# Attention, max-of-three layer and gated layer on one core: two weight pairs put together in PSUM banks of the row products, half products in other banks, every second output copy on ScalarE

## The chip, the cores and the metric

One core of a Trainium2 chip runs the whole program once. The metric is device time in microseconds (us), the median of several runs. The engines of the core are named as the profile names them: PE (TensorE, the matrix unit; PEld is its weight load), DVE (VectorE), ACT (ScalarE), POOL (GpSimd) and SP (SyncE, which here only issues DMAs). Matrix products land in PSUM, of which there are eight banks of 128 x 512 fp32; everything else lies in SBUF.

## The reference, cut to what matters

Attention over 2 batches, 8 heads, 768 positions and head width 64, in which a query sees the 8 global positions and the 96 positions behind it; then a layer with the largest of three products; then a normalised, gated layer.

```python
scores = np.matmul(q, k.transpose(0, 1, 3, 2)) / np.sqrt(64)
# keep = (pos < n_global) | ((0 <= rel) & (rel < n_local)); a bias falls linearly with distance
a = softmax(where(keep, scores + bias, -1e9))
x = np.matmul(a, v)                                   # as 1536 tokens x 512

h = np.maximum(np.maximum(x @ w1, x @ w2), x @ w3)    # 512 -> 768
x = h @ w_out                                         # 768 -> 512

xn = x / sqrt(mean(x * x) + 1e-6) * rms_g
g, val = xn @ w_gate, xn @ w_val                      # 512 -> 1536
out = (g / (1 + exp(-g)) * val) @ w_out2              # 1536 -> 512
```

## The kernel before

**Numbers.** Every fp32 operand of a large product is held as two parts, a rounded one and the rest (`op[:, 0]`, `op[:, 1]`), and a product is three matrix products of such parts. The weights come as 64-bit numbers and are put together on the chip: `scaled` (L131) lets ACT scale the high words into a buffer `x`, and `bits` (L148) has three DVE steps, L152 (shift), L154 (or with the low words, `raw`) and L160 (sign). The buffer of the first two steps is a PSUM bank where `self.psx` is set (its tile is then called `xs`) and SBUF otherwise.

**Stages.** (1) Attention, 24 units `d` (a pair of heads, 256 queries) in rounds, with the first products of the second layer (`mm`, L473) put in between. Per round DVE does the normaliser `rs` (L1095, L1096), a copy `xf` of an older unit's output out of PSUM (L1153), four score rows with their maximum (L1083), a copy `at` (L1120) and one or two weight steps; ACT does four exponentials (L1087), the copies `xt` (L1148) and `at` (L1118) and weight steps; POOL scales the probabilities (L1101), takes `xt`'s rest (L1155) and splits weights (L174). (2) The remaining products of the max-of-three layer, by a scheme with seven products in place of eight (`chained`, L689), 49 of them. (3) `behind` (L893): twelve row products `mo` of 18 matmuls (L558), each 128 tokens wide. Before one runs, its hidden rows are split by `row_part` (L538): ACT casts (L542), then DVE (part 0, and part 1 of the first row) or POOL (part 1 of the others) takes the rest `rst` (L544). After one has run, ACT squares it (L571), DVE averages (`ms`, L576), POOL takes the root (`ri`, L578), DVE scales (`x`, L582), PE transposes (`tr`, L592), and DVE, ACT and POOL make seven sums of it (`xb`, L596 to L613). (4) `gated`: 14 half products `q` for the first hidden block (`second`, L619), then 77 products `c` (L703), then the output products `acc` (L820) and stores.

**Order.** In the stages 1, 2 and 4 the order on each engine is the program's. In stage 3 only PE keeps it; the other engines are placed by a planner, from the same dependences. Between the stages 2 and 3 DVE also holds `sums1` (L711), which closes the last maximum `h_1` (L733 to L755) that row 0 needs.

**What the change touches.** `pace` (L119) takes one more step of weight work, `operand` (L302) splits one of the seven combinations of a weight pair (ACT L314, POOL L315), and `mixed` (L271) first forms four of these by sums (L282; on POOL for the max-of-three weights, on DVE for gated ones, numbered `f` >= 0). In stage 3 the banks come from `single` (L442), six of them in three pools of two; `bank` (L438) gives one of two other banks, used there for the transposes.

## Time and profile before

| | us |
|---|---|
| median of 3 runs (566.63 to 568.32) | 566.73 |
| the profiled execution's own time | 566.71 |
| its span, first to last instruction | 564.8 |
| PE busy | 546.7 (97%) |
| DVE busy | 381.4 (68%) |
| ACT busy | 292.0 (52%) |
| POOL busy | 314.7 (56%) |

The granted TensorE clock was 0.998 of full speed over the span. The page's slices show where PE is not full: PE stands at 9 tenths in nearly all of 40 slices and at 6 in the one slice from 226 to 240 us, where stage 2 ends and stage 3 starts; DVE stands at 9 there and in the slices from 14 to 56 us. A row of a timeline gives the start, the busy time, the engine, the line and the tile written and read; what stands in brackets is how long the engine sat idle before it and what ended that.

### The profile page before, as it was taken

The page shows a single profiled execution, that of the slowest core. Times are in us where ns is not written, and L with a number is a line of the kernel's source. Part 1 is how long each engine was busy: PE and PEld are TensorE (multiplying, and loading weights), DVE is VectorE, ACT ScalarE, POOL GpSimd, SP SyncE. Part 2 cuts the span into 40 slices and gives each one's busy share as a digit, 9 for nine tenths or more (in the row PEclk, how much of TensorE's full clock was granted, in tenths as well). Part 3 has the DMA queues.
Part 4 walks back from the last instruction along what each step waited for, and adds up shares of the span by engine and source line. Part 5 has one row for each costly group of instructions (what it writes and reads, how often), then busy time and mean ns, then how long its engine had stood idle before and what let it go on. Part 6 is the DMA issues. An engine that isn't in the chain of part 4 may idle for free.

```text
span 564.8 us, 9257 instructions
## 1 busy us (share of the span) xinstructions
PE 546.7 (97%) x3240; PEld 495.2 (88%) x3240; DVE 381.4 (68%) x788; ACT 292.0 (52%) x684; POOL 314.7 (56%) x397
## 2 busy tenths in 40 slices
PE   8988999999999999699999999999999999999995
PEld 4667887899999999588899999999999998888884
DVE  5999899578767768977687555555556359662220
ACT  4887768445644552566565555554444455442210
POOL 4679688666755771676746666666666527320000
PEclk9999999999999999999999999999999999999999
DMA  8666551102422432220001122222222205203101
GB/s 295 209 227 196 165 202 39 38 1 75 149 76 75 126 99 75 75 75 1 0 1 29 54 72 72 76 75 74 76 75 74 75 5 180 77 1 131 38 20 43
DMA packets 15896, 48.74 MB, mean 86 GB/s; under 512 B 2016, under 2 KB 2016, under 8 KB 15840
## 3 DMA queue, kind: packets, MB, share of 16 engines
q1 hardware_dynamic: 15840, 48.05, 26.5%
q8 instruction: 28, 0.46, 0.3%
q14 instruction: 28, 0.23, 0.1%
HBM read 44.90 MB, written 3.15 MB: 85 GB/s over the span
## 4 chain that ended last, share of the span: by engine, by line
PE 81%; DVE 14%; ACT 2%; issue 1%; POOL 1%; DVEq 0%; ACTq 0%; POOLq 0%
PE c L703 28%; PE acc L820 17%; PE mo L558 7%; PE mm L473 4%; DVE s L1083 3%; PE sc L1070 2%; PE av L1134 2%; PE tr L1111 2%; PE c_-2_0_2680 L703 1%; PE c_-3_0_2529 L703 1%; PE c_-4_0_2384 L703 1%; PE c_-5_0_2229 L703 1%; PE c_-6_0_2078 L703 1%; PE c_-7_0_1966 L703 1%; DVE x L160 1%
## 5 line engine op out<-in xcount | busy, mean ns | idle before, releaser
L703 PE MATMUL c<-xb,op 128*128 128x384 f32 x924 | 160.4, 334 | 0.2 <-DVE g L645 0.2
L703 PEld LDWEIGHTS c<-xb,op 128*128 128x128 f32 x924 | 160.1, 188 | 0.5 <-POOL op L315 0.5
L315 POOL TENSOR_TENSOR op<-s,op 128x256 fp32r<-128x256 f32 x48 | 39.3, 821 | 32.6 <-ACT op L314 31.5
L558 PE MATMUL mo<-w,rst 128*128 128x512 f32 x216 | 52.7, 396 | 2.9 <-DVE rst L544 2.9
L1101 POOL TENSOR_SCALAR s<-s,rs 128x232 f32<-128x232 f32 (+1 forms) x96 | 41.8, 454 | 20.3 <-DVE rs L1096 11.1
L1087 ACT ACTIVATE s<-s,nmx 128x232 f32<-128x232 f32 (+1 forms) x96 | 44.5, 466 | 14.4 <-DVE nmx L1083 14.2
L558 PEld LDWEIGHTS mo<-w,rst 128*128 128x128 f32 x216 | 39.6, 188 | 11.7 <-issue 2.1
L820 PE MATMUL acc<-w,gst 128*128 128x512 f32 x216 | 49.2, 389 | 0.0
L820 PE MATMUL acc<-w,st 128*128 128x512 f32 x216 | 49.1, 389 | 0.0
L820 PEld LDWEIGHTS acc<-w,st 128*128 128x128 f32 x216 | 40.5, 188 | 8.4
L820 PEld LDWEIGHTS acc<-w,gst 128*128 128x128 f32 x216 | 40.5, 188 | 8.4
L174 POOL TENSOR_TENSOR w<-x,w 128x512 fp32r<-128x512 f32 x22 | 32.3, 1466 | 26.7 <-ACT w L171 26.7
L315 POOL TENSOR_TENSOR op<-x,op 128x256 fp32r<-128x256 f32 x36 | 28.9, 806 | 28.9 <-ACT op L314 27.6
L769 POOL TENSOR_TENSOR h<-h,g 128x768 f32<-128x768 f32 x20 | 36.9, 1847 | 12.3 <-ACT g L787 10.0
L152 DVE TENSOR_SCALAR xs<-xs 128x512 int32<-128x512 int32 x48 | 33.2, 691 | 8.7 <-ACT xs L140 8.5
L790 DVE TENSOR_TENSOR h<-c,h 128x768 f32<-128x768 f32 x11 | 10.5, 957 | 41.8 <-PE c L703 41.8
L473 PE MATMUL mm<-xt,w 128*128 128x384 f32 x192 | 37.7, 343 | 0.6 <-ACT h L488 0.6
L160 DVE SCALAR_TENSOR_TENSOR x<-raw,xs 128x512 int32<-128x512 int32 x48 | 32.8, 684 | 2.9
L1070 PE MATMUL sc<-qk 64*128 64x232 f32 (+1 forms) x192 | 28.8, 377 | 5.7 <-DVE nmx L1083 5.4
L473 PEld LDWEIGHTS mm<-xt,w 128*128 128x128 f32 x192 | 32.6, 188 | 1.3 <-ACT h L488 1.0
L154 DVE SCALAR_TENSOR_TENSOR xs<-raw,xs 128x512 int32<-128x512 int32 x48 | 33.1, 690 | 0.9
L1083 DVE CUSTOM_DVE_ANT_0 s<-sc,bias 128x232 f32<-128x232 f32 (+1 forms) x96 | 31.5, 375 | 0.6 <-PE sc L1070 0.2
(453 smaller groups left out, 1108.4 us busy)
## 6 DMA issues: line engine op xcount, KB each, us to landing
raw<-wgv SPq DMA_DIRECT2D x24, 512.0 KB, 3.6
raw<-w SPq DMA_DIRECT2D x18, 512.0 KB, 3.9
raw<-wo SPq DMA_DIRECT2D x18, 512.0 KB, 3.6
qk<-qk SPq DMA_DIRECT2D x24, 312.0 KB, 4.0
v<-vwin SPq DMA_DIRECT2D x10, 512.0 KB, 4.7
out<-o SPq DMA_DIRECT2D x12, 256.0 KB, 2.1
v<-vwin SPq DMA_DIRECT2D x2, 256.0 KB, 3.9
gcol<-gcol SPq DMA_DIRECT2D x1, 2.0 KB, 1.6
```

The lines of the kernel that those rows point to most:

```text
L152: nc.vector.tensor_scalar(x, x, 3, 0x7FFFFFFF, op0=ALU.logical_shift_left, op1=ALU.bitwise_and)
L160: nc.vector.scalar_tensor_tensor(out=self.x[i].bitcast(I32), in0=raw[:, :, 1], scalar=-(1 << 31), in1=x, op0=ALU.bitwise_and, op1=ALU.bitw ...
L315: nc.gpsimd.tensor_tensor(out=t[:, 1, :], in0=s, in1=t[:, 0, :], op=ALU.subtract)
L473: self.nc.tensor.matmul(ps, w[:, wi, k * P:(k + 1) * P], x[b][:, k, xi, c0:c0 + C2], start=(i == 0), stop=(i == 3 * KT - 1),)
L558: self.nc.tensor.matmul(ps, h[:, k % 3, hi, :], w[:, wi, :], start=(k + x == 0), stop=(k == NF1 - 1 and x == 2),)
L703: nc.tensor.matmul(two[:, b, :C2], a[:, wi, k * P:(k + 1) * P], x, start=(i == 0 and j in (0, 1, 5)), stop=(i == 5), skip_group_check=True,)
L769: nc.gpsimd.tensor_tensor(out=o, in0=o, in1=y, op=ALU.mult)
L820: self.nc.tensor.matmul(ps, of(si), w[:, wi, :], start=(f == LAST[0] and si == 1), stop=(f == LAST[-1] and si == 0 and wi == 0),)
L1070: nc.tensor.matmul(sc[j][:, i, :n], qk[r, i * P:(i + 1) * P], qk[r, k0:k0 + n], start=True, stop=True)
L1083: nc.vector.tensor_tensor_reduce(out=s[:, j, :n], in0=self.sc[d][j][:, i, :n], in1=self.bias(n, 2 * pr + j), scale=-QK, scalar=3.0e38, op0 ...
L1087: nc.scalar.activation(s[:, j, :n], s[:, j, :n], AF.Exp, bias=nmx[:, j:j + 1], scale=-1.0, accum_out=sm[:, i, j:j + 1])
L1101: nc.gpsimd.tensor_scalar(s[:, j, :n], s[:, j, :n], rs[:, i, j:j + 1], 1.0, op0=ALU.mult, op1=ALU.mult)
```

## The change

There are five edits. The attention's `xf` copies of odd units go from DVE to ACT. The weight buffers `x` come from one pool of four instead of two pools of two. In `behind`, weight pairs 1 and 2 (gate and value) are put together in a PSUM bank of the first of the three row-product pools (`psx` with tag `m1`), pair 1 from the third row on and pair 2 from the sixth, instead of in SBUF from the first row on; pair 0's seven operands are appended to `order` and issued there too. The sums of pair 0 go from DVE to POOL (`f <= 0`). And in `second` the last two products of the second half (`j > 4`) take their banks from `bank`, with the rotation of the two-bank pools started one further (`n_bank = 1`).

```diff
@@ -101,11 +101,11 @@
         e = ctx.enter_context
         self.rawp = e(tc.tile_pool(name="rawp", bufs=NRAW))
         self.sp = e(tc.tile_pool(name="sump", bufs=3))
-        self.xp = [e(tc.tile_pool(name="xp0", bufs=2)), None]
+        self.xp = e(tc.tile_pool(name="xp", bufs=4))
         self.ops = self.psx = self.xone = None
         self.w, self.places, self.x, self.raws = {}, {}, {}, {}
         self.done, self.held, self.in_psum = set(), set(), set()
-        self.blocked, self.mix = False, {}
+        self.blocked, self.mix, self.psx_tag = False, {}, "mm"
         self.run = self.everything()
 
     def __getitem__(self, key):
@@ -132,7 +132,7 @@
 
 
         if self.psx is not None:
-            x = self.psx.tile([P, 512], F32, tag="mm", name=f"xs_{i}")
+            x = self.psx.tile([P, 512], F32, tag=self.psx_tag, name=f"xs_{i}")
             self.in_psum.add(i)
         else:
             x = self.xof(i).tile([P, 512], F32, tag="x", name=f"x_{i}")
@@ -140,10 +140,7 @@
         self.nc.scalar.activation(x, self.raws[i][:, :, 1].bitcast(F32), AF.Copy, scale=2.0 ** -112)
 
     def xof(self, i):
-        key, _, place = self.units[i]
-        if place == "wo1":
-            return self.xone
-        return self.xp[(key[1] if place == "op" else i) % 2]
+        return self.xone if self.units[i][2] == "wo1" else self.xp
 
     def bits(self, i, part):
         nc = self.nc
@@ -278,7 +275,7 @@
 
         def of(x, y, op):
             s = self.sp.tile([P, h], F32, tag="s", name=f"s_{f}_{j}")
-            eng = self.nc.gpsimd if -NA < f < 0 else self.nc.vector
+            eng = self.nc.gpsimd if -NA < f <= 0 else self.nc.vector
             eng.tensor_tensor(out=s, in0=x, in1=y, op=op)
             return s
 
@@ -343,7 +340,6 @@
             {q: xtp.tile([P, 2, C2], F32, tag=f"xf{b}{q[0]}{q[1]}", name=f"xf_{b}{q[0]}{q[1]}") for q in QUARTERS}
             for b in range(B)
         ]
-        self.weights.xp[1] = e(tc.tile_pool(name="xp1", bufs=2))
         self.ring_only = ExitStack()
         ring = self.ring_only.enter_context(tc.tile_pool(name="ring", bufs=RING))
         self.weights.places["ring"] = (ring, "w")
@@ -400,7 +396,6 @@
         self.thi_one.close()
         self.two_only.close()
         self.weights.psx = None
-        self.weights.xp[1] = self.ctx.enter_context(self.tc.tile_pool(name="xp2", bufs=2))
         e, tc = self.rows_only.enter_context, self.tc
         self.singles = [e(tc.tile_pool(name=f"m1{n}", bufs=2, space=PSUM, side="right")) for n in range(3)]
         self.rowp = e(tc.tile_pool(name="rowp", bufs=4, side="right"))
@@ -418,7 +413,7 @@
         self.rows_only.close()
         self.open_twos()
         e, tc = self.ctx.enter_context, self.tc
-        self.weights.psx = self.mm0
+        self.weights.psx, self.weights.psx_tag = self.mm0, "mm"
         h2b = e(tc.tile_pool(name="h2b", bufs=1, side="right"))
         self.h2.append(h2b.tile([P, NF1, NT], F32, tag="h", name="h2_2"))
         self.weights.places["wo2a"] = (e(tc.tile_pool(name="wo2a", bufs=1, side="right")), "wo2")
@@ -624,7 +619,7 @@
         a = self.weights["op", f, j]
         for b in range(b0, b1):
             later.step()
-            ps = self.single("q_" + nm, C2)
+            ps = (self.bank if b and j > 4 else self.single)("q_" + nm, C2)
             i = 0
             for k in range(2):
                 for wi, xi in ((1, 0), (0, 1), (0, 0)):
@@ -841,7 +836,8 @@
     def next_op(self):
         if self.n_op < len(self.order):
             self.n_op += 1
-            self.weights.operand(*self.order[self.n_op - 1], (self.order + [None])[self.n_op])
+            then = None if self.n_op in (self.n_first, len(self.order)) else self.order[self.n_op]
+            self.weights.operand(*self.order[self.n_op - 1], then)
 
     def begin(self):
 
@@ -851,6 +847,8 @@
         for o in range(1 - NA, z):
             self.order += [(o, 0), (o - 1, 4), (o - 1, 6), (o, 1), (o, 2), (o, 5), (o, 3)]
         self.order += [(z, 0), (z - 1, 4), (z, 2), (z - 1, 6), (z, 3), (z, 5), (z, 1), (z, 6), (z, 4)]
+        self.n_first = len(self.order)
+        self.order += [(0, j) for j in range(7)]
 
     def strassen(self):
 
@@ -873,10 +871,10 @@
         later.flush()
         self.open_strassen()
         self.rst, done = {}, 0
-        for n, (o, j) in enumerate(self.order):
+        for n, (o, j) in enumerate(self.order[:self.n_first]):
             later.step()
             for b, _ in enumerate(self.chained(o, j)):
-                if b == 0:
+                if b == 0 and self.n_op < self.n_first:
                     self.next_op()
                 h = 2 * (n % 7) + b + 1
                 paces = min(-(-PACES[n // 7] * max(h - 2 * (n < 7), 0) // (8 if n < 7 else 10 if PACES[n // 7] == 6 else 14)), PACES[n // 7])
@@ -895,22 +893,21 @@
 
         w = self.weights
         self.open_second()
-        n_op = 0
         for t in range(NT // P):
+            w.psx, w.psx_tag = self.singles[0], "m1"
             for n, _ in enumerate(self.rows(t)):
-                if ("x", 1) in w.done and n_op < 7:
-                    w.operand(0, n_op)
-                    n_op += 1
-                elif ("x", 2) not in w.done:
+                if t > (1 if ("x", 1) not in w.done else 4) and ("x", 2) not in w.done:
                     w.pace()
+                if t > 1:
+                    self.next_op()
                 if n == 0 and t + 1 < NT // P:
                     self.row_stage(t + 1)
 
                 if n == 2 and t:
                     self.norm(t - 1)
-        while n_op < 7:
-            w.operand(0, n_op)
-            n_op += 1
+        while self.n_op < len(self.order):
+            self.next_op()
+        w.need(("x", 2))
 
     def gated(self):
 
@@ -935,6 +932,7 @@
                 pass
         later.flush()
         self.open_gated()
+        self.n_bank = 1
         for n, (f, j) in enumerate(order):
             later.step()
             for b, _ in enumerate(self.chained(f, j)):
@@ -1150,7 +1148,10 @@
         for q, n, i in self.places(b, pr, c):
             a = slice(i * P, i * P + n)
             if part == 1:
-                nc.vector.tensor_copy(q, av[:, a])
+                if d % 2:
+                    nc.scalar.copy(q, av[:, a])
+                else:
+                    nc.vector.tensor_copy(q, av[:, a])
             elif not last:
                 nc.gpsimd.tensor_tensor(out=o[:, 1, a], in0=q, in1=o[:, 0, a], op=ALU.subtract)
         if part == 1 and last:
```

What the planner makes of it on DVE, where stage 2 ends: the rows are those from the last maximum of the max-of-three layer to the second row's `rst`. Before:

```order
L735 TENSOR_TENSOR h_1_1864<-u_-1_1_2858,h_1_1864 128x2x384
L752 TENSOR_TENSOR u_-1_2_2894<-c_-1_5_2930,u_-1_2_2894 128x768
L282 TENSOR_TENSOR s_2_3163<-s_2_3161,x_2923 128x256
L733 TENSOR_TENSOR h_1_1864<-u_-1_2_2894,h_1_1864 128x384 x2
L282 TENSOR_TENSOR s_4_3217<-x_2923,s_2_3163 128x256
L152 TENSOR_SCALAR x_3045<-x_3045 128x512
L152 TENSOR_SCALAR x_3060<-x_3060 128x512
L154 SCALAR_TENSOR_TENSOR x_3045<-raw_2925,x_3045 128x512
L544 TENSOR_TENSOR rst_1_2995<-h_1_1864,rst_1_2995 128x3x128
L750 TENSOR_TENSOR h_1_1864<-c_-1_0_2838,h_1_1864 128x2x384
L282 TENSOR_TENSOR s_5_3228<-x_2923,x_2953 128x256
L154 SCALAR_TENSOR_TENSOR x_3060<-raw_2955,x_3060 128x512
```

The same place on DVE in the changed kernel (its lines are numbered three to five lower here):

```order
L730 TENSOR_TENSOR h_1_1861<-u_-1_1_2855,h_1_1861 128x2x384
L747 TENSOR_TENSOR u_-1_2_2891<-c_-1_5_2927,u_-1_2_2891 128x768
L728 TENSOR_TENSOR h_1_1861<-u_-1_2_2891,h_1_1861 128x384 x2
L539 TENSOR_TENSOR rst_1_2992<-h_1_1861,rst_1_2992 128x3x128
L745 TENSOR_TENSOR h_1_1861<-c_-1_0_2835,h_1_1861 128x2x384
L539 TENSOR_TENSOR rst_0_3038<-h_0_128,rst_0_3038 128x3x128
L539 TENSOR_TENSOR rst_0_3066<-h_0_128,rst_0_3066 128x3x128
L571 TENSOR_SCALAR ms_3078<-sq_3064 128x1
L577 TENSOR_SCALAR x_0_3063<-mo_3031,ri_3080 128x512
L539 TENSOR_TENSOR rst_0_3120<-h_0_128,rst_0_3120 128x3x128
L149 TENSOR_SCALAR xs_3115<-xs_3115 128x512
L151 SCALAR_TENSOR_TENSOR xs_3115<-raw_2922,xs_3115 128x512
```

All weight rows (`x`, `raw`) and the four sums `s` are gone from between the maxima and `rst`; the first weight rows now stand behind the first row's scaling `x_0`, and they write `xs`.

The same place on POOL, from the first split operand of pair 0 to the first row's root. Before:

```order
L315 TENSOR_TENSOR op_1_3152<-x_2923,op_1_3152 128x256
L315 TENSOR_TENSOR op_2_3165<-s_2_3163,op_2_3165 128x256
L315 TENSOR_TENSOR op_3_3201<-s_2_3161,op_3_3201 128x256
L544 TENSOR_TENSOR rst_1_3050<-h_1_1864,rst_1_3050 128x3x128
L315 TENSOR_TENSOR op_4_3219<-s_4_3217,op_4_3219 128x256
L315 TENSOR_TENSOR op_5_3230<-s_5_3228,op_5_3230 128x256
L315 TENSOR_TENSOR op_6_3259<-x_2953,op_6_3259 128x256
L544 TENSOR_TENSOR rst_1_3086<-h_1_1864,rst_1_3086 128x3x128
L578 TENSOR_TENSOR ri_3097<-ms_3095,mhalf 128x1
```

And on POOL in the changed kernel:

```order
L312 TENSOR_TENSOR op_1_3140<-x_2920,op_1_3140 128x256
L279 TENSOR_TENSOR s_2_3136<-x_2950 128x256
L279 TENSOR_TENSOR s_2_3138<-s_2_3136,x_2920 128x256
L279 TENSOR_TENSOR s_4_3191<-x_2920,s_2_3138 128x256
L312 TENSOR_TENSOR op_2_3150<-s_2_3138,op_2_3150 128x256
L312 TENSOR_TENSOR op_3_3193<-s_2_3136,op_3_3193 128x256
L312 TENSOR_TENSOR op_4_3212<-s_4_3191,op_4_3212 128x256
L279 TENSOR_TENSOR s_5_3210<-x_2920,x_2950 128x256
L539 TENSOR_TENSOR rst_1_3041<-h_1_1861,rst_1_3041 128x3x128
L312 TENSOR_TENSOR op_5_3225<-s_5_3210,op_5_3225 128x256
L312 TENSOR_TENSOR op_6_3254<-x_2950,op_6_3254 128x256
L573 TENSOR_TENSOR ri_3080<-ms_3078,mhalf 128x1
```

The four sums `s` stand on POOL now, three of them ahead of every split that needs them, and the second row's `rst_1` stands behind seven rows instead of two.

## Rows read from the trace of the kernel before

**Rows 1.** Chain of work that ended last: start us, us, what.

```profile
239.38 4.13 PE mo L558 x18
...
300.30 160.42 PE c L703 x924
```

**Rows 2.** Waits of PE, whole span: waiter <- releaser: us, times, longest.

```profile
PE sc L1070 <- DVE nmx L1083: 5.4, 8, 1.7
...
PE c L703 <- DVE g L645: 0.2, 1, 0.2
```

**Rows 3.** Timeline of PE where stage 3 starts.

```profile
225.50 2.25 PE L558 MATMUL mo<-w,rst 128*128 128x512 f32 x9
228.88 2.36 PE L558 MATMUL mo<-w,rst 128*128 128x512 f32 x9 [1.13 <-DVE rst L544]
232.98 4.34 PE L558 MATMUL mo<-w,rst 128*128 128x512 f32 x18 [1.74 <-DVE rst L544]
238.73 0.66 PE L592 MATMUL tr<-ident,x 128*128 128x128 f32 x4 [1.41 <-DVE x L582]
```

**Rows 4.** Timeline of DVE there.

```profile
226.67 0.41 DVE L282 TENSOR_TENSOR s<-x,s 128x256 f32<-128x256 f32 x1
227.01 0.75 DVE L152 TENSOR_SCALAR x<-x 128x512 int32<-128x512 int32 x2
227.68 0.68 DVE L154 SCALAR_TENSOR_TENSOR x<-raw,x 128x512 int32<-128x512 int32 x1
228.28 0.55 DVE L544 TENSOR_TENSOR rst<-h,rst 128x384 fp32r<-128x384 f32 x1
228.75 0.95 DVE L750 TENSOR_TENSOR h<-c_-1_0_2838,h 128x768 f32<-128x768 f32 x1
229.62 0.80 DVE L282 TENSOR_TENSOR s<-x,x 128x256 f32<-128x256 f32 x1
230.34 1.50 DVE L154 SCALAR_TENSOR_TENSOR x<-raw,x 128x512 int32<-128x512 int32 x1
231.76 1.07 DVE L544 TENSOR_TENSOR rst<-h,rst 128x384 fp32r<-128x384 f32 x1
```

**Rows 5.** Timeline of POOL: a sum in stage 2, then two splits where stage 3 starts.

```profile
207.38 0.74 POOL L282 TENSOR_TENSOR s_-1_4_2845<-x,s_-1_2_2716 128x256 f32<-128x256 f32 x1
...
227.32 2.81 POOL L315 TENSOR_TENSOR op<-s,op 128x256 fp32r<-128x256 f32 x2 [6.92 <-ACT op L314]
```

**Rows 6.** Timeline of ACT: a cast of `rst` there.

```profile
229.00 0.52 ACT L542 CAST rst<-h 128x384 fp32r<-128x384 f32 x1
```

**Rows 7.** Stretches: a:b length, PE busy (x) PEld DVE ACT POOL busy, clock, DMA share, GB/s.

```profile
17.94:47.56 29.62, 25.44 (x241) 19.80 (x240) 29.09 (x109) 24.27 (x83) 22.77 (x43) 1.00 0.63 204
47.56:67.59 20.03, 20.03 (x183) 16.42 (x183) 18.12 (x68) 16.14 (x60) 16.35 (x31) 1.00 0.54 173
...
239.10:262.00 22.90, 22.90 (x114) 18.91 (x112) 17.42 (x38) 15.56 (x41) 16.37 (x15) 1.00 0.16 50
```

**Rows 8.** Timelines of DVE and ACT in one round of the attention.

```profile
37.39 0.46 DVE L1153 COPY xf<-av 128x128 f32<-128x128 f32 x2
37.76 0.39 DVE L1083 CUSTOM_DVE_ANT_0 s<-sc,bias 128x232 f32<-128x232 f32 x1
...
38.20 0.49 ACT L1087 ACTIVATE s<-s,nmx 128x232 f32<-128x232 f32 x1 [1.84 <-DVE nmx L1083]
```

**Rows 9.** One line's durations over the span, ns min/median/max: ACT's copy `xt`.

```profile
L1148 ACT CAST xt<-av x24: 347/357/374, 18.4 to 112.3; 128x256 fp32r<-128x256 f32 x24
```

**Rows 10.** The same for the weight step in a PSUM bank.

```profile
L152 DVE TENSOR_SCALAR xs<-xs x48: 682/690/700, 127.5 to 495.2; 128x512 int32<-128x512 int32 x48
```

**Rows 11.** Timelines of DVE and PE in the fourth and fifth row of stage 3.

```profile
246.62 0.74 DVE L582 TENSOR_SCALAR x<-mo,ri 128x512 f32<-128x512 f32 x1
...
247.92 0.60 PE L592 MATMUL tr<-ident,x 128*128 128x128 f32 x4
```

## The prediction

> **What bounds the kernel now.** I read the chain of waits first. From 300.30 us on it is PE alone, 924 `c` matmuls in 160.42 us and then the output products [rows 1]; the changed kernel has the same matmuls there, so time can only come from what lies before 300 us. Next I read the waits of PE over the whole span: little is listed before 220 us but 5.4 us for DVE's score rows [rows 2]. Third, the timeline of PE where stage 3 starts. Row 0's first nine matmuls start at 225.50; then PE waits 1.13 us for `rst`, 1.74 us before row 1 for `rst`, and 1.41 us for the scaled row `x` before the first transposes, at 238.73 [rows 3]. A whole product takes 4.13 us back to back [rows 1], so two of them would have ended at 225.50 + 8.26 = 233.76: the seam loses 238.73 - 233.76 = 4.97 us, a little more than the three waits, since PE refills after each. Last, the timeline of DVE there: it never rests, and between its rows of `rst` stand weight rows and sums that nobody needs yet [rows 4].
>
> **The attention copies.** Twelve of 24 `xf` copies leave DVE. From 17.94 to 47.56 us DVE is busy 29.09 of 29.62 us and PE only 25.44, so DVE's queue sets the pace; from 47.56 to 67.59 PE is busy throughout [rows 7], and a copy taken from DVE there gives nothing. Four of the twelve stand in the first stretch. One holds DVE from 37.39 to the next row at 37.76, 0.37 us [rows 8], so 4 x 0.37 = 1.5 us come off. ACT takes 0.36 us for a piece of that shape [rows 9], 1.4 us for four; it has 29.62 - 24.27 = 5.35 us free there [rows 7], and in the round shown it sits idle for 1.84 us before the exponentials [rows 8]. That idle time is the cover; without it a copy would delay the exponentials by its 0.36 us and the gain would be gone. ACT does not idle in each round, so I take 1.2 us. Bounds: a loss of 0.5 (one or two copies uncovered and nothing gained), and 2.2 (six copies instead of four pay).
>
> **The seam, DVE's part.** Ahead of row 0's second `rst` the removed rows are those from 226.67 to 228.28, 1.61 us, and two more sums like the first of them, which takes 0.34 from start to start [rows 4]: 2.3 us in all. DVE would finish the last maximum before it at 226.67 - 0.68 = 226.0; ACT's cast takes 0.52 [rows 6], DVE's `rst` 0.55 [rows 4], with hand-overs 227.2. PE wants it at 227.75, when its nine matmuls end [rows 3]. So the first wait would vanish. Ahead of row 1's `rst`, the sum of 0.80 and the weight row of 1.50 are removed too [rows 4]: what is left between the two is the maximum at 228.75, 0.87 from start to start, so this `rst` would end some 1.5 us behind the first, while PE still works on nine matmuls. For the third wait: row 0's square, `ms`, root and scaling take some 3 us from its end, and row 1 hides 4.13 of work [rows 1].
>
> **The seam, POOL's part.** The four sums are not gone, they are on POOL, 0.74 us each where it has the same form [rows 5]; there POOL was idle for 6.92 us [rows 5], so its own time is covered. But two rows of DVE stretch exactly where POOL works: the sum at 229.62 takes 0.80 against 0.41 at 226.67, the `rst` at 231.76 takes 1.07 against 0.55 at 228.28, and POOL's two splits take 2.81 where a like row takes 0.74 [rows 4, 5]. Up to now POOL slept while DVE closed the maxima; now POOL's seven rows lie on them. Three DVE rows of two SBUF operands (one L735, two L733) and `rst` could each wait for one POOL row of 0.74. Bounds for row 0's second half: no delay, and 4 x 0.74 = 3.0 us behind 227.2, a wait of 2.4. The stretched rows grew by 0.4 to 0.5, about half a POOL row, so I take that for the three maxima, 3 x 0.37 = 1.1, and 0.1 for one more hand-over: `rst` at 228.4, and PE waits 228.4 - 227.75, about 0.7 us, once and not at the other two places. The seam then loses 0.7 of 4.97: a gain of 4.3 us, between 2.5 (a wait of 2.4) and 5.0. The Trainium skill has a rule against this edit: "Perfetto Trace Analysis", section "Optimizing Scalar/DVE Operations", says that GpSimd and DVE share an SBUF read port, so work moved between the two may not help. Here its sum would be the low one; the stretched rows agree with it, the removed 2.3 us speak against it.
>
> **The rows after the seam.** The two weight pairs are four `x` of three steps, twelve rows; in a PSUM bank a step takes 0.69 [rows 10], 8.3 us. Part of that stood behind 239.1 already (four rows, some 2.6 us), so 5 rows of stage 3 get about 5.7 more. DVE was busy 17.42 of 22.90 us there [rows 7]; 23.1 would be over full, but starts lie 0.60 apart where rows last 0.69, and two of the twelve fall ahead of the first transposes: some 21 of 22.9. The cover of one row product: `x` ends at 246.62 + 0.74 = 247.36 and the transposes start at 247.92, a slack of 0.56 [rows 11]. One weight step of 0.6 before it just uses that up, two do not fit. Such a wait hits five rows at most: between 0 and 2.0 us, and I take 0.8. A bank that is shared also has to be read before the next product needs it, but a pool's turn comes once in three rows, 3 x 4.13 = 12.4 us, so that is 0.
>
> **The rest.** The half products in `bank` take away what holds the first `c`, 0.2 us [rows 2]; 0 to 0.2, I take 0.2. The pool of four buffers holds as many as the two pools did: 0, and if a pair had to wait for a buffer, the 0.56 of slack is its cover. The deferred loads of weights run on a queue with 0.16 of DMA in use [rows 7]: 0.
>
> **The sum.** 1.2 + 4.3 - 0.8 + 0.2 = 4.9 us. The profiled execution took 566.71 us, span 564.8 and 1.9 around it, which is also the median of the three runs within 0.02; 566.7 - 4.9 = 561.8.
>
> **Rivals.**
> (1) *POOL takes DVE's place.* The sums on POOL and the maxima on DVE block each other row by row; the seam yields 2.5 and the total is 1.2 + 2.5 - 0.8 + 0.2 = 3.1: 563.6. For it: the stretched rows. Against it: DVE's rows that read PSUM beside one SBUF operand keep their length (0.95 at 228.75, in the middle of POOL's 2.81) [rows 4, 5].
> (2) *The copies give nothing*, since ACT or POOL is late next in the attention: 566.7 - 3.7 = 563.0. For it: POOL is busy 22.77 of 29.62 [rows 7] and PE's listed waits are short.
> (3) *All is covered.* 2.2 + 5.0 + 0.2 = 7.4: 559.3.
> (4) *Slower: the rows become bound by DVE.* The twelve weight steps stand ahead of `x` in rows 1 to 5 and none of them is hidden: 1.2 + 4.3 + 0.2 - 8.3 = -2.6, 569.3. It decides from the point where DVE has more than 0.56 us of new work between a product's end and its `x` in each row. For it: 21 of 22.9 us. Against it: only one step or two stand there in a row.
> (5) *It does not do what it says*: the wait is handed to ACT's cast or POOL's `rst` at the same place, and only a part of the copies is left: 566.0.
>
> **How the numbers follow.** Forecast 0.48 (560.6 to 562.8), (1) 0.20, (2) 0.10, (3) 0.10, (4) 0.05, (5) 0.07. The range from 559.6 to 565.2 leaves out (4), (5) and a little of (3): it takes the unknown costs' bounds, 2.2 + 5.0 at the good end and 0.4 + 2.5 - 1.6 + 0.2 at the bad one. About 0.3%, 1.7 us, is what a measurement can tell from no change: faster than 565.0 holds the forecast, (1), (2) and (3) and loses a little at their ends, 0.86; (5) and that rest give 0.09; (4) gives 0.05.
>
> **What would show it.** In the changed profile: row 0's second half following its first with a wait under 1 us and no wait before row 1; the first transposes about 8.5 to 9 us behind row 0's start instead of 13.2; the `c` of stage 2 starting some 1.2 us earlier; waits of PE for `x` in rows 2 to 5 that add up to less than 1 us; `xs` steps of 0.69 in stage 3. Wrong would be: POOL rows of 1.4 us beside stretched maxima and a wait over 2 us for `rst` (1); attention that ends as late as before (2); a wait of PE for `x` before every transposes (4).

## The result, and the profile after

The changed kernel takes 560.81 us (median of 4 runs, 560.70 to 560.90) against 566.75 for the kernel before in the same session: a ratio of 0.989, 95% interval 0.9874 to 0.9906. The forecast was 561.8, its range 559.6 to 565.2. The profiled execution took 560.9 us with a span of 559.0, against 566.71 and 564.8.

Of the changed kernel, the chain of waits (start us, us, what), which answers to [rows 1]:

```profile
294.68 160.16 PE c L698 x924
454.84 97.97 PE acc L815 x432
```

The `acc` products start 460.72 - 454.84 = 5.88 us earlier than before, where the chain had `c` end at 300.30 + 160.42 [rows 1]. That is the whole gain (the spans differ by 5.8).

Its waits of PE over the span (us in total, times, longest), which answer to [rows 2]; L1068 was L1070, L553 was L558, L587 was L592:

```profile
PE sc L1068 <- DVE nmx L1081: 4.1, 6, 1.4
...
PE mo L553 <- DVE rst L539: 0.8, 1, 0.8
...
PE tr L587 <- DVE x L577: 0.3, 1, 0.3
```

The wait of the first `c` for `g` is gone, and two of the three waits at the seam are.

Its timelines of PE, DVE and POOL where stage 3 starts, which answer to [rows 3], [rows 4] and [rows 5] (start us, us, engine, line, form; in brackets the idle time before and what ended it):

```profile
223.66 2.25 PE L553 MATMUL mo<-w,rst 128*128 128x512 f32 x9
226.71 6.45 PE L553 MATMUL mo<-w,rst 128*128 128x512 f32 x27 [0.81 <-DVE rst L539]
233.01 0.60 PE L587 MATMUL tr<-ident,x 128*128 128x128 f32 x4
...
279.42 3.37 PE L626 MATMUL q<-xb,op 128*128 128x384 f32 x18
```

```profile
221.61 1.32 DVE L730 TENSOR_TENSOR h<-u_-1_1_2855,h 128x768 f32<-128x768 f32 x1
222.85 0.94 DVE L747 TENSOR_TENSOR u_-1_2_2891<-c_-1_5_2927,u_-1_2_2891 128x768 f32<-128x768 f32 x1
223.83 1.83 DVE L728 TENSOR_TENSOR h<-u_-1_2_2891,h 128x384 f32<-128x384 f32 x2
225.58 1.08 DVE L539 TENSOR_TENSOR rst<-h,rst 128x384 fp32r<-128x384 f32 x1
```

```profile
222.19 1.34 POOL L279 TENSOR_TENSOR s<-x,s 128x256 f32<-128x256 f32 x1
223.49 2.75 POOL L312 TENSOR_TENSOR op<-s,op 128x256 fp32r<-128x256 f32 x3
```

From row 0's first `mo` to its transposes the seam takes 233.01 - 223.66 = 9.35 us, before 238.73 - 225.50 = 13.23 [rows 3]. The weight rows and sums are gone from DVE. POOL now works beside the last maxima, and the rows of DVE that overlap it are the long ones: L728, two rows, takes 1.83 and `rst` 1.08 (0.55 in [rows 4]).

Split by place, the gain is this. Attention: row 0 starts at 223.66 instead of 225.50, **1.84**; stage 2 between is the same dense work. Seam: 13.23 - 9.35 = **3.88**. Rows, from the first transposes to the first `q`: 279.42 - 233.01 = 46.41 us; before, `q` started at 284.81 in the trace, 284.81 - 238.73 = 46.08, so **-0.33**. First `q` to `acc`: 454.84 - 279.42 = 175.42 against 460.72 - 284.81 = 175.91, **0.49** (the chain's starts of `acc`; the timelines have them 0.16 sooner in both kernels). The sum is 5.88.

### The profile page after: what moved, and what is told of

Same layout as the page of the kernel before. It is cut to its first block, busy times and chain, and to the rows that moved or that the text cites. A ratio compares the mean times of both kernels' runs of the same rounds, so it can differ in the third digit from the quotient of the medians.

```text
span 559.0 us, 9249 instructions
## 1 busy us (share of the span) xinstructions
PE 545.6 (98%) x3240; PEld 494.8 (89%) x3240; DVE 374.4 (67%) x768; ACT 295.2 (53%) x700; POOL 316.7 (57%) x401
## 4 chain that ended last, share of the span: by engine, by line
PE 84%; DVE 8%; ACT 4%; POOL 2%; issue 1%; ACTq 0%; POOLq 0%; DVEq 0%
PE c L698 29%; PE acc L815 18%; PE mo L553 6%; PE mm L468 4%; PE sc L1068 3%; PE q L626 3%; PE tr L1109 2%; PE av L1132 2%; DVE s L1081 2%; ACT s L1085 2%; PE c_-2_0_2677 L698 1%; PE c_-3_0_2526 L698 1%; PE c_-4_0_2381 L698 1%; PE c_-5_0_2226 L698 1%; PE c_-6_0_2075 L698 1%; PE c_-7_0_1963 L698 1%
## 5 line engine op out<-in xcount | busy, mean ns | idle before, releaser
L553 PE MATMUL mo<-w,rst 128*128 128x512 f32 x216 | 52.4, 396 | 0.8 <-DVE rst L539 0.8
L553 PEld LDWEIGHTS mo<-w,rst 128*128 128x128 f32 x216 | 39.7, 188 | 9.2 <-DVE rst L539 1.2
L149 DVE TENSOR_SCALAR xs<-xs 128x512 int32<-128x512 int32 x52 | 35.9, 691 | 9.5 <-ACT xs L140 9.3
L157 DVE SCALAR_TENSOR_TENSOR x<-raw,xs 128x512 int32<-128x512 int32 x52 | 35.5, 683 | 2.8
L151 DVE SCALAR_TENSOR_TENSOR xs<-raw,xs 128x512 int32<-128x512 int32 x52 | 35.9, 691 | 1.0
L140 ACT ACTIVATE xs<-raw 128x512 f32<-128x512 f32 x52 | 32.5, 632 | 3.4 <-DMA raw<-wo 3.1
```

Of the source, the lines that this page charges most:

```text
L149: nc.vector.tensor_scalar(x, x, 3, 0x7FFFFFFF, op0=ALU.logical_shift_left, op1=ALU.bitwise_and)
L151: nc.vector.scalar_tensor_tensor(out=x, in0=raw[:, :, 0], scalar=29, in1=x, op0=ALU.logical_shift_right, op1=ALU.bitwise_or)
L157: nc.vector.scalar_tensor_tensor(out=self.x[i].bitcast(I32), in0=raw[:, :, 1], scalar=-(1 << 31), in1=x, op0=ALU.bitwise_and, op1=ALU.bitw ...
L553: self.nc.tensor.matmul(ps, h[:, k % 3, hi, :], w[:, wi, :], start=(k + x == 0), stop=(k == NF1 - 1 and x == 2),)
```

## The experiments

Each kernel is the changed one with one more edit, or two where it says so. Below, "attention" is the start of the first `c` of stage 2 in the timeline of PE (123.58 before, 121.74 changed; the chain shows it 0.16 later), "seam" and "rows" are as above.

**e1_copies_back.** The copies back on DVE.

```diff
-                if d % 2:
+                if False:
                     nc.scalar.copy(q, av[:, a])
```

> The changed kernel with all xf copies on DVE again; nothing else differs. Theory A (the copies gave the whole 1.84 us by which the attention ended earlier, and nothing else in the change bears on it): the first c of stage 2 goes from 121.90 back to 123.74 us, the time from 560.8 to 562.6, the seam (223.66 to 233.01 from row 0's start to the first transposes, 9.35 us) stays as it is. Rival B (the pool of four x buffers or the order of weight steps gave part of it): the first c starts between 122.3 and 123.3. By A the rows rs of four elements take 0.156 to 1.78 us as before, 12.6 us for 24, and three of them between 72 and 89 us are the long ones (1.77, 1.78, 1.38).

Measured: 564.33 us, more than theory A allowed. Three of its four times lie within 564.28 to 564.43, and one is 562.94, 0.3 us above theory A's 562.6; the profiled execution is one of the three. The attention ends at 125.14, which is 1.56 us past before's. From 8.5 to 47.6 us its rounds start where before's do, within 0.03 us; then one round takes 5.78 us instead of 4.24. Its timeline of PE at that round, with the same row of the kernel before under it, and its stretches (length, then busy us of PE, PEld, DVE, ACT, POOL, then PE's granted clock, DMA share, GB/s):

```profile
47.59 1.20 PE L1068 MATMUL sc<-qk 64*128 64x128 f32 x8 [1.48 <-DVE nmx L1081]
47.56 1.20 PE L1070 MATMUL sc<-qk 64*128 64x128 f32 x8 [1.47 <-DVE nmx L1083]
```

```profile
47.59:50.00 2.41, 2.41 (x16) 2.09 (x17) 2.38 (x8) 1.95 (x8) 1.97 (x5) 0.81 0.41 118
50.00:52.00 2.00, 2.00 (x8) 1.82 (x7) 2.00 (x10) 2.00 (x9) 2.00 (x5) 0.50 0.42 144
```

The granted clock fell to 0.50, the 1.2 GHz level, after PE had waited 1.48 us for the score rows: 2.00 us hold 8 matmuls. In the kernel before the same wait is 1.47 and the same stretch has 23 matmuls:

```profile
50.00:52.00 2.00, 2.00 (x23) 1.57 (x23) 2.00 (x10) 1.82 (x10) 2.00 (x5) 1.00 0.41 144
```

Taking the 1.54 us of that round off, the attention ends at 123.60, and before's is 123.58. Behind that round the two kernels' rounds are again alike within 0.04 us. So the copies gave the 1.84 us and the pool of four gave nothing: theory A holds, with a clock loss on top. Why the clock falls here, and not in the kernel before beside the same rows, is not shown.

**e2_no_add.** Without the row that adds 1e-9.

```diff
-        nc.vector.tensor_scalar(rs, sm, 1e-9, None, op0=ALU.add)
-        nc.vector.reciprocal(rs, rs)
+        nc.vector.reciprocal(rs, sm)
```

> The changed kernel without DVE's row that adds 1e-9 to the sums (L1093): the reciprocal reads them directly. A sum holds the term exp(0) = 1 of its largest score, so 1e-9 is below its last bit. In the changed kernel this row has four elements a partition and takes 0.156 to 1.43 us, 11.3 us for 24, and each long one ends with a POOL row. Theory S (the row is what POOL's rows hold up, and takes back part of what the copies free): 6 to 7.5 us of DVE's time go with it in the attention, PE has 5 to 9 us above its dense time there, ACT is next; the first c starts 2 to 4 us earlier than 121.90, the time is 557 to 559. Rival R (POOL's rows then hold up the next DVE row of two SBUF operands, or the exponentials are late anyway): the first c moves by less than 0.8 us, the time is 560.0 to 561.

Why this row: the six copy rows (of four units) taken from DVE in the first stretch, 1.70 us, should have given all of their time and gave 0.63 us. The stretches with only this line's instructions (a:b length, DVE busy and count, then clock, DMA share, GB/s), of before and then of the changed kernel; the bounds are starts of the same three rounds:

```profile
17.94:47.56 29.62, 3.44 (x8) 1.00 0.63 204
47.56:91.00 43.44, 8.18 (x10) 1.00 0.47 151
```

```profile
17.94:46.93 28.99, 4.53 (x8) 1.00 0.64 202
46.93:89.20 42.27, 5.59 (x10) 1.00 0.49 160
```

Eight rows of four elements a partition take 4.53 us. The copies there fell from 3.40 to 1.70 us in the same view, `rs` rose by 1.09: what is left, 0.61, is about the 0.63 that the stretch got shorter. Further on it is the other way round. A long `rs` of before on DVE, and beside it POOL:

```profile
82.11 1.78 DVE L1095 TENSOR_SCALAR rs<-sm 128x4 f32<-128x4 f32 x1 [0.50 <-ACT s L1087]
```

```profile
82.03 1.84 POOL L520 TENSOR_TENSOR xf<-xf,xf 128x768 f32<-128x768 f32 x1
```

Both end at 83.9. In the changed kernel the row of the same round comes just before POOL's `mix` instead of just behind its start:

```profile
80.64 0.27 DVE L1093 TENSOR_SCALAR rs<-sm 128x4 f32<-128x4 f32 x1 [0.50 <-ACT s L1085]
```

```profile
80.84 1.84 POOL L515 TENSOR_TENSOR xf<-xf,xf 128x768 f32<-128x768 f32 x1
```

In the two traces 8 and 13 of the 24 `rs` rows last over 0.3 us. Each of these 21 starts while a POOL row is running and ends 0.02 to 0.03 us behind it. The reciprocal that follows (also four elements) is never longer than 0.18 us, not even the four in the changed kernel that lie inside a POOL row. The Trainium skill, "SBUF — State Buffer", section "Who interferes with whom", names `tensor_scalar` among the operations that can take the port pair which GpSimd uses, and says that whoever issues first has the pair for its whole instruction while the other fully blocks. The 21 rows agree with it.

Measured: 557.77 us (ratio to before 0.9833, 0.9814 to 0.9852), the attention ends at 118.62, 3.12 us earlier than in the changed kernel. Theory S holds: the first stretch, now 17.51 to 43.99, takes 26.48 us, 2.51 less, where the eight rows that are gone would be 1.3 at their shortest, 0.16 each. PE's wait for the score rows shrinks:

```profile
PE sc L1068 <- DVE nmx L1081: 1.5, 3, 1.1
```

**e3_no_add_copies_back.** The same with the copies on DVE: the two diffs above together.

> As e2_no_add, with all xf copies on DVE: what the copies are worth where DVE has no such row. Theory S (with the copies gone, rs rows stretch by 1.09 us in 17.9 to 47 us and give back over half of the 1.86 us that six copies took there): without rs the copies are worth their full 0.31 us each in the rounds that DVE bounds, so this kernel ends the attention 2 us or more later than e2_no_add. Rival M (between 72 and 89 us the copies gained only because rs fell outside POOL's long rows): without rs this gain of 1.2 us is not there, and this kernel is 0.6 us or less behind e2_no_add.

Measured: 558.90 us, the attention ends at 119.70, 1.08 us behind the last kernel: between the two theories. From 74 us on, in the rounds where the copies had gained 1.2 us, the two kernels' rounds are equal (4.09, 5.13, 4.09, 4.09 us). So M's number holds there: without `rs` the copies are worth nothing in these rounds. M's reason is not shown by it. PE has no wait there in either of these two kernels, so they say only that DVE was late with `rs`; whether the copies' own time or the shift of the rows behind them gained the 1.2 us stays open. The first stretch can't be read: here too the clock fell, to 0.52 from 40.30 to 42.81 us, and in e2_no_add POOL, busy 4.71 of 4.71 us in the round from 43.99 on, takes back a part. How much the copies are worth there without `rs` stays open.

**e4_all_act.** All copies on ACT.

```diff
-                if d % 2:
+                if True:
                     nc.scalar.copy(q, av[:, a])
```

> The changed kernel with all 24 units' xf copies on ACT. From 17.94 to 46.93 us ACT is busy 25.37 of 28.99 us, six more copies of some 0.31 us make it 27.2. Theory A (a copy off DVE pays while DVE bounds the round and ACT has room): the first c starts 0.3 to 1.0 us before 121.90, the time is 559.8 to 560.5. Rival C (ACT is now late for the exponentials, which each round needs): the first c starts 0.3 to 1.5 us later, 561.1 to 562.3.

Measured: 558.84 us (ratio 0.9852, 0.9833 to 0.9871), attention 119.69, 2.05 us earlier than changed: twice theory A's best, and rival C is out. The first stretch of 28.99 us becomes 26.14. That is more than the 1.70 us of six more copy rows, since the `rs` rows there fall from 4.53 to 2.92 us: moved copies shift them this way too. The round behind it is now POOL's (columns as in the stretches above):

```profile
17.92:44.06 26.14, 25.10 (x242) 19.27 (x241) 25.27 (x99) 25.59 (x94) 22.74 (x40) 1.00 0.65 208
44.06:49.36 5.30, 4.57 (x41) 3.28 (x39) 4.67 (x16) 4.45 (x19) 5.30 (x10) 1.00 0.61 224
```

POOL is busy 5.30 of 5.30 us there, in a round that took 4.24 in the changed kernel: 1.06 us of the 2.85 that the first stretch gained are given back.

**e5_sums_dve.** The sums on DVE.

```diff
-            eng = self.nc.gpsimd if -NA < f <= 0 else self.nc.vector
+            eng = self.nc.gpsimd if -NA < f < 0 else self.nc.vector
```

> The changed kernel with the four sums of pair 0 on DVE again, the weight pairs as they are. Three of the sums then stand ahead of row 0's second rst on DVE, 0.34 us each from start to start in the kernel before. Theory P (POOL is the better place): the wait before row 0's second half grows from 0.81 to about 1.8 us, the seam (first mo of row 0 to the first transposes) from 9.35 to 10.3, the time from 560.8 to 561.8. Rival B (the sums on POOL hold up DVE's rows of two SBUF operands by as much as they take off: L730 1.32 us beside POOL against 0.96 alone, L728 1.83 against 1.02 for two, rst 1.08 against 0.55): the seam stays between 9.1 and 9.6 and the time within 0.3 us.

Measured: 561.04 us, the seam is 9.81, 0.46 more: between the two. The seven traces with the seam as in the changed kernel have 9.35 to 9.37, so this is clear of their scatter; the time grows by 0.23 only, since in this trace the attention ends 0.25 earlier without an edit there. Its DVE and PE at the seam:

```profile
223.64 1.02 DVE L728 TENSOR_TENSOR h<-u_-1_2_2891,h 128x384 f32<-128x384 f32 x2
224.58 0.41 DVE L279 TENSOR_TENSOR s<-x,s 128x256 f32<-128x256 f32 x1
224.97 1.04 DVE L539 TENSOR_TENSOR rst<-h,rst 128x384 fp32r<-128x384 f32 x1
```

```profile
226.06 2.32 PE L553 MATMUL mo<-w,rst 128*128 128x512 f32 x9 [0.41 <-DVE rst L539]
229.02 4.37 PE L553 MATMUL mo<-w,rst 128*128 128x512 f32 x18 [0.63 <-DVE rst L539]
```

The first wait is even smaller than with the sums on POOL, since L728 is not stretched; a second one comes before row 1. POOL is the better place, by half a microsecond of the 3.88.

**e6_late_pool.** POOL's rows of pair 0 behind the `rst` of row 1.

```diff
+            with self.behind(f): eng.tensor_tensor(out=s, in0=x, in1=y, op=op)
...
+        with self.behind(f): nc.gpsimd.tensor_tensor(out=t[:, 1, :], in0=s, in1=t[:, 0, :], op=ALU.subtract)
+    def behind(self, f): return self.tc.issue_after(self.mark) if f == 0 and self.mark else nullcontext()
```

> The changed kernel with POOL's eleven rows of pair 0 (four sums, seven splits) issued behind its rst of row 1, so that nothing of POOL lies beside DVE's last maxima. Theory L (the wait of 0.81 us that is left at the seam is the stretch of L728 and rst beside POOL, 0.81 + 0.53 us): L728 falls to 1.0 us for two and rst to 0.55, the wait falls below 0.2, the seam from 9.35 to between 8.3 and 8.7, the time to 560.0 to 560.2. Rival H (the casts of ACT and the hand-overs set the rst, or the late rows hold up the root ri of row 0): the wait stays over 0.5, or a new wait of over 0.5 stands before the transposes, and the time is 560.5 or more.

`mark` is POOL's `rst` of row 1. Measured: at the seam all that L says, in the whole time the opposite. Timeline of DVE and PE:

```profile
223.27 1.03 DVE L728 TENSOR_TENSOR h<-u_-1_2_2891,h 128x384 f32<-128x384 f32 x2
224.41 0.56 DVE L539 TENSOR_TENSOR rst<-h,rst 128x384 fp32r<-128x384 f32 x1
```

```profile
223.46 8.37 PE L553 MATMUL mo<-w,rst 128*128 128x512 f32 x36
231.67 0.60 PE L587 MATMUL tr<-ident,x 128*128 128x128 f32 x4
...
237.51 0.66 PE L587 MATMUL tr<-ident,x 128*128 128x128 f32 x4 [1.12 <-DVE x L577]
```

36 matmuls without a wait, the seam at 8.21. But the time is 561.56 us: the rows take 48.43 instead of 46.42. Row 1's transposes wait 1.12 us, since its root `ri` stands behind POOL's late rows (it starts at 235.97, `x` at 236.71); 0.58 more are lost in rows 4 and 5. So the remaining wait at the seam is POOL's, as L says, and H is right that its rows are not free elsewhere.

**e7_pairs_sbuf.** The pairs in SBUF.

```diff
-            w.psx, w.psx_tag = self.singles[0], "m1"
+            w.psx = None
```

> The changed kernel with the weight pairs 1 and 2 put together in SBUF, all else (pace, pool of four, sums on POOL) as changed. A bank of the row products is free only when stage 2 has ended; an SBUF buffer is free earlier, and in this kernel's order six weight rows stand between DVE's maxima ahead of row 0's second rst. Theory G (the bank works as a gate, and that is most of the seam's gain): six rows of 0.4 to 0.75 us put the rst 2.5 to 4 us later, the seam is 11.5 to 13.5 instead of 9.35, the time 563 to 565. Rival T (it is the later turn in the program that counts): the seam stays below 10 and the time below 561.3.

Measured: 568.68 us, slower than before (1.0025, 1.0013 to 1.0036); the seam is 17.92. PE:

```profile
232.37 9.23 PE L553 MATMUL mo<-w,rst 128*128 128x512 f32 x27 [6.61 <-DVE rst L539]
```

Seven weight rows and the stretched maxima stand between 220.5 and 231.8 us on DVE, and after 6.61 us of waiting the clock is 0.50 from 232 to 236, so 27 matmuls take 9.23 us where 6.45 were enough. Without these 2.78 us the seam would be 15.1, still longer than before's 13.23. Theory G holds and had its price too low: the later turn in the program alone keeps nothing away, since the planner pulls the rows forward. ACT scales the first words of pairs 1 and 2 into an SBUF buffer at 217.12, 6.4 us ahead of the end of stage 2 at 223.51; into the bank, in the next kernel, at 228.06, 4.7 behind that end.

**e8_pairs_early.** The pairs in the bank, but from row 0 on.

```diff
-                if t > (1 if ("x", 1) not in w.done else 4) and ("x", 2) not in w.done:
+                if ("x", 2) not in w.done:
```

> The changed kernel with the weight pairs in the PSUM bank, but their steps taken from row 0 on as before the change. In its order six rows xs of 0.69 us stand behind row 2's rst and ahead of row 0's scaling x. Theory G (the bank alone keeps the weight rows out of the maxima, the later turn keeps them away from row 0's scaling): the wait before row 0's second half stays at 0.8, a new one of 1 to 2.5 us stands before the first transposes, since x of row 0, which ended 1.45 us before PE wanted it, is put off by three to six rows of 0.69; the seam is 10.3 to 12, the time 561.8 to 563.5. Rival T (all of it is cover): the seam stays below 9.8, the time below 561.3.

Measured: 562.19 us, seam 10.83, as theory G says:

```profile
226.45 6.42 PE L553 MATMUL mo<-w,rst 128*128 128x512 f32 x27 [0.80 <-DVE rst L539]
234.23 0.66 PE L587 MATMUL tr<-ident,x 128*128 128x128 f32 x4 [1.35 <-DVE ms L571]
```

The first wait is that of the changed kernel; the second is six `xs` rows ahead of row 0's `x`. Beside the bank the later turn is worth 10.83 - 9.35 = 1.48 us; without the bank (e7_pairs_sbuf) it does not help.

**e9_single_bank.** The last half products in the row products' banks.

```diff
-            ps = (self.bank if b and j > 4 else self.single)("q_" + nm, C2)
+            ps = self.single("q_" + nm, C2)
...
-        self.n_bank = 1
+        self.n_bank = 0
```

> The changed kernel with the last half products back in the row products' banks and the two-bank pools' turn as before. From the first half product q to the first output product acc the kernel before takes 15.49 + 160.26 = 175.75 us, the changed one 15.10 + 160.16 = 175.26, 0.49 us less; only 0.2 of it is listed as a wait of PE. Theory K (the banks are all of it): this stretch is 175.7 again, the wait of the first c for g is back, the time is 561.2 to 561.4. Rival N (the lighter DVE of the stretch gave it): the stretch stays below 175.4, the time within 0.15 us of 560.8.

Measured: 561.35 us. By the timelines the stretch is 175.74 again (175.75 before, 175.26 changed), and PE's wait is back:

```profile
294.97 1.28 PE L698 MATMUL c<-xb,op 128*128 128x384 f32 x6 [0.24 <-DVE g L640]
```

Theory K: the banks gave all of the 0.49, half of which no list of waits shows.

**e10_no_add_all_act.** The diffs of e2_no_add and e4_all_act together.

> e2_no_add and e4_all_act together: no row that adds 1e-9, all xf copies on ACT. Alone they ended the attention 3.12 and 2.05 us earlier than the changed kernel (118.62 and 119.69 against 121.74). Theory O (POOL bounds by now: it is busy 4.71 of 4.71 and 5.30 of 5.30 us in the round from 44 us on of these two): together they give at most 0.7 us more than e2_no_add alone, the first c at 118.0 to 118.6, the time 557.2 to 557.8. Rival S (DVE still bounds, so the gains add up): the first c at 117.3 or earlier, 556.5 or less.

Measured: 557.32 us, ratio to before 0.9842 (0.9813 to 0.9872), attention 118.19: theory O by its numbers. Three of its four times lie within 557.23 to 557.34, one is 559.66. This is the fastest kernel of the study, 3.5 us under the changed one. Its stretches:

```profile
17.70:42.99 25.29, 24.86 (x241) 18.94 (x240) 22.78 (x91) 24.82 (x92) 22.27 (x40) 1.00 0.67 220
42.99:48.28 5.29, 4.71 (x41) 3.50 (x39) 4.39 (x16) 4.89 (x20) 5.29 (x11) 1.00 0.64 218
```

DVE, 29.09 of 29.62 us before [rows 7], is down to 22.78 of 25.29; ACT is at 24.82 now, and POOL fills the round behind. Theory O's reason holds only in part: in the attention PE's listed waits are 0.8 us for POOL's probabilities, none of which e2_no_add has, and 0.9 for DVE's score rows, and in the first stretch PE itself is busy 24.86 of 25.29 us.

**e11_spread.** POOL's rows of pair 0 thinned out over rows 2 to 8. The diff of the late rows with the mark set in each row, and one operand a row:

```diff
-                if t > 1:
+                if t > 1 and n == 1:
                     self.next_op()
```

> The changed kernel with pair 0's seven operands formed one a row, rows 2 to 8, and their POOL rows issued behind the rst of the row that follows. In e6_late_pool the seam fell to 8.21 us, but POOL's eleven rows stood in rows 0 to 2 then, and the rows from the first transposes to the first q grew from 46.42 to 48.43. Theory L (what was lost there is the root ri waiting behind POOL's rows, and goes when they are thinned out): the seam stays at 8.2, the rows take 46.1 to 46.7, the time is 559.5 to 559.9. Rival H (eleven POOL rows cost PE their 1 to 2 us wherever they stand in stage 3, since each stretches DVE's rows): the rows take 47.4 or more, the time is 560.6 or more.

Measured: 569.90 us. The seam is 8.21 as hoped, the rows take 55.38:

```profile
243.62 0.63 PE L587 MATMUL tr<-ident,x 128*128 128x128 f32 x4 [2.72 <-DVE ms L571]
244.00 6.00 PE L553 MATMUL mo<-w,rst 128*128 128x512 f32 x18
```

The root of row 2 came behind two POOL rows, its `x` on DVE behind sums and a split of the row before, three of whose rows took 0.96, 0.96 and 1.31 us beside POOL. PE's five waits before transposes in these rows add up to 6.8 us; and the clock fell after the wait, to 0.50 from 246 to 248 us, so 18 matmuls took 6.00 us instead of 4.37. The rival's price was right in sign and far too low.

**e12_part_late_best.** The fastest kernel, with only six POOL rows late.

```diff
+            with self.behind(f, j - 3): eng.tensor_tensor(out=s, in0=x, in1=y, op=op)
...
+    def behind(self, f, j): return self.tc.issue_after(self.mark) if f == 0 and j > 1 and self.mark else nullcontext()
```

> e10_no_add_all_act (557.32 us), and of pair 0's POOL rows only the six that stood beside DVE's last maxima and the rst (the splits of operands 2 to 6 and the sum of operand 5) are issued behind the rst of row 1; the other five stay early. Theory L (the 0.81 us of wait at the seam is the stretch of L728 and rst beside just these rows; fewer late rows than in e6_late_pool leave the root ri in time): the seam falls from 9.36 to 8.2 to 8.5, the rows from the first transposes to the first q take 46.1 to 46.8, the time is 556.1 to 556.5. Rival H (late POOL rows cost the rows 1 to 2 us, as 48.43 in e6_late_pool and 55.38 in e11_spread): the rows take 47.4 or more, the time is 557.2 or more.

Measured: 558.17 us, seam 8.23, rows 48.19. Now it is not the root. PE waits in rows 4 and 5, the longer time here, and DVE and POOL beside it:

```profile
253.57 0.66 PE L587 MATMUL tr<-ident,x 128*128 128x128 f32 x4 [1.31 <-DVE x L577]
```

```profile
250.39 0.69 DVE L157 SCALAR_TENSOR_TENSOR x<-raw,xs 128x512 int32<-128x512 int32 x1
251.00 1.85 DVE L592 TENSOR_TENSOR xb<-z,xb 128x768 fp32r<-128x768 f32 x1
252.77 0.74 DVE L577 TENSOR_SCALAR x<-mo,ri 128x512 f32<-128x512 f32 x1
```

```profile
251.98 2.00 POOL L592 TENSOR_TENSOR xb<-y,xb 128x512 fp32r<-128x512 f32 x1
```

With row 0 earlier the planner orders pair 2's steps otherwise; three of them and a split that takes 1.85 beside POOL (0.95 at its shortest in these rows) stand ahead of `x`. That is the prediction's rival (4), in one row. A kernel that keeps both the seam at 8.2 and the rows at 46.4 was not found.

## Why the prediction was right, and where its steps were not

**What bounds the kernel** held: PE alone from `c` on, and the whole gain lies before it or at its start.

**The attention copies: 1.2 predicted, 1.84 measured,** inside the bounds; that a copy off DVE pays where DVE sets the pace was right, the place was not. The working took 4 x 0.37 us in the stretch to 47.56 and said that a copy gives nothing behind it, because PE is busy throughout up to 67.59 [rows 7]. The first stretch gave 0.63, since `rs` took back 1.09. The other 1.2 came from three rounds between 75 and 91 us (0.51, 0.31 and 0.39), which the working never looked at: there PE waits for the score rows twice in the kernel before and once in the changed one.

```profile
80.75 1.37 PE L1070 MATMUL sc<-qk 64*128 64x232 f32 x8 [0.32 <-DVE nmx L1083]
90.95 1.37 PE L1070 MATMUL sc<-qk 64*128 64x232 f32 x8 [0.61 <-DVE nmx L1083]
```

```profile
89.11 1.37 PE L1068 MATMUL sc<-qk 64*128 64x232 f32 x8 [0.22 <-DVE nmx L1081]
```

Ahead of the first wait DVE has a copy that the change moves (0.39 us) and a weight row that overlaps a POOL row and ends some 0.55 us behind it in both kernels, before and then changed:

```profile
76.73 2.40 DVE L160 SCALAR_TENSOR_TENSOR x<-raw,x 128x512 int32<-128x512 int32 x1
```

```profile
75.19 1.12 DVE L157 SCALAR_TENSOR_TENSOR x<-raw,x 128x512 int32<-128x512 int32 x1
```

Ahead of the second stand another moved copy (0.46) and an `rs` of 1.38, 0.90 in the changed kernel. The `rs` of 1.78 shown under e2_no_add stands ahead of no wait: PE's next scores, at 86.19, follow without one. So the failed steps of this term are to look for the gain in one stretch alone and to price a removed row at its own duration. A removed row also shifts those behind it into or out of POOL's rows. In the first stretch this took back 1.09 of 1.70 us. How much of the 1.2 us is the two copies' own 0.85 and how much the shorter rows, no run separates.

**The seam: 4.3 predicted, 3.88 measured.** The steps held, with two small errors that cancel. The wait before row 0's second half is 0.81 (0.7 predicted), the `rst` ends 226.66 - 223.66 = 3.0 us behind row 0's start (2.9 predicted), and there is none of the other two waits. Without POOL beside it (e6_late_pool) this `rst` ends 1.5 us behind row 0's start, where the prediction had 1.7, so POOL put it off by 1.5 and not by 1.2; that the sum came out at 2.9 is partly luck. The term that was mis-sized is PE's refill after the wait that remains: two rows without a wait take 8.21 in e6_late_pool, with the 0.81 they take 9.35, so 0.33 more is lost. The prediction named this loss for the kernel before and left it out for the one after. What the prediction did not know is which edit does the work: the bank first, the later turn only beside it, as e7_pairs_sbuf and e8_pairs_early show.

**POOL's part** was weighed right in the balance. Both the hold-up of DVE's rows beside POOL and the gain from moving the sums are there: the rows L730, L728 and `rst` stretch by 0.36, 0.81 and 0.53 us against their lengths without POOL, and yet the sums on POOL are 0.46 better than on DVE. Rival (1) is real in mechanism, and its price was too high.

**The rows: 0.8 predicted, 0.33 measured,** one wait of 0.26 in twelve rows; most steps fit the slack. Rival (4) did not come, but e6_late_pool, e11_spread and e12_part_late_best show how near it is: 2.0, 9.0 (with a fall of the clock) and 1.7 us were lost in the rows there by changes of order alone.

**The rest: 0.2 predicted, 0.49 measured.** The list of waits had only 0.2 of it; the banks were worth over twice that.

**The sum.** 1.84 + 3.88 - 0.33 + 0.49 = 5.88 against 4.9. The errors are +0.64, -0.42, +0.47 and +0.29, so the near hit is partly luck: one of them points the other way. The range's ends are not the bounds that were worked out: 2.2 + 5.0 gives 559.5, not 559.6, and the bad end takes 0.4 and -1.6 where the working had bounds of -0.5 for the copies and -2.0 for the rows; with those it would have been 566.7, no gain at all. Rivals (2), (3) and (5) are out: the copies gave 1.84, the seam kept a wait, and no engine took the place of the ones relieved.

## What to carry to other kernels

A row taken from a busy engine is worth its duration plus or minus what the rows behind it now collide with; look for tiny rows with long durations (here 128x4 elements, 0.16 to 1.78 us), see what ends together with them, and whether the bounding engine waits behind them, before moving anything else. With a planner that pulls work forward, where a buffer lies decides when work can start: here a bank that is free late kept it away from a critical place, and a later line in the program helped only beside it. And sum all stretches in which the bounding engine waits, not just the first one.

## What was not expected of the hardware

A DVE row of four elements a partition was held up to 1.78 us by a single POOL row, and ended 0.02 to 0.03 us behind it in 21 of 21 long cases.

TensorE's granted clock fell to 0.50 (1.2 GHz) for a stretch in or behind waits of 1.48, 1.47, 2.72 and 6.61 us in e1_copies_back, e3_no_add_copies_back, e11_spread and e7_pairs_sbuf, and did not after one of 1.47 in the kernel before, with the same work around it as in the first of these. The cost of a fall differed: 1.54 us in e1_copies_back's round, 1.63 in 18 matmuls of e11_spread, 2.78 in 27 of e7_pairs_sbuf, all on top of the wait. In the attention of e11_spread the clock also stood at 0.50 from 40.2 to 43.5 us, behind a wait of 1.41, and nothing was lost: the two rounds there, with DVE busy 4.49 of 4.56 us in the first, take 8.56 us, and 8.57 in the changed kernel, which waits 1.41 at the same place and keeps its clock. What decides whether it falls was not settled.
